# New step orders for all four stages of a state-space and gate kernel with its gradients

## The chip, the core and the metric

The kernel runs on one core of a Trainium2 chip. A core has five engines, each with its own queue of instructions that it works off in order: TensorE (PE in the profile; its weight loads are PEld), VectorE (DVE), ScalarE (ACT), GpSimd (POOL) and SyncE (SP, which here only issues transfers). They meet only at semaphores. TensorE writes its results to PSUM, and DVE or ACT must copy them out ("evict" them) before the bank can be used again. The metric is the device time of one execution in microseconds; the median of the runs counts.

## What is computed

The reference is a forward pass and its gradients. Cut to what matters:

```python
xn = layernorm(x)                              # x: [1, 2048, 512]
K[d, l] = Re sum_n C * exp(dt*A*l) * dt*B      # SSM kernel, 512 channels, 128 states, 2048 lags
s = causal_conv(xn, K) + xn * Dskip            # by FFT of length 4096
g = silu(silu(xn @ w1) @ w2)                   # w1: 512x1792, w2: 1792x512
out = x + s * g
# returned: out, and the gradients of sum(out * grad_out) with respect to
# x, A_re, A_im, B_re, B_im, C_re, C_im, log_dt, Dskip, w1, w2
```

## The kernel before

The program is unrolled and its schedule is manual: the order in which the Python code issues instructions is the order in which every engine's queue gets them. Four functions follow each other.

- **stage_1** (first step order): layer norm (`Setup.stats`, `.norm`, `.param`), the powers of exp(dt*A) (`power_phases`: X, XV, A, B, C, CC, S; B is three ACT passes, A and C are DVE work), and the two matrix products of the gate (`gen_ffn_fwd`). One step of the latter, an h step, makes 128x1024 of x@w1 in a PSUM tile ps_h, takes SiLU of it on ACT (aT) and copies it too (hs).
- **stage_2**: for four blocks b of channels, the tables of powers X and CY are loaded, copied on ACT (`copy_tables`, L869 and L870, step c) and multiplied out on DVE (`chunk_tables` and `quads`, L884 to L905, step g, five steps a block); TensorE makes K from them (`chunk_K`, step k, 4 a block), and transposes X (`gen_xt`, tile XT, step t, 11 a block). Beside that run the transform of xn (`spectrum`, step u: per half 8 steps of FA, a transpose on DVE (L162, 2 x 2.3 us), 8 steps of FX) and the transposes of w2 (step w, tile w2o). Step o opens the tables of a further block: transfers on the SP queue into the two table buffers, which have to be free. At its end K is stored (`store_K`), and stage_3 changes the PSUM banks and reads K again in another layout (`load_K`).
- **stage_3**: transforms of K and of the incoming gradient, their products, and the inverse transforms. DVE multiplies and transposes, ACT and DVE evict.
- **stage_5**: gradients of w2 (`Dw2`, step w, tile KXW), of h (`Bwd.dh`, step h, with the transposed result dhk), of x (`Bwd.dx`, step x), of the state tables (`Slabs`, step l: P2 twice, with the eviction Vb, then D3 on DVE, L1649 and L1652; the last step is P3, which needs the last D3), of w1 (`grads`, step m, tile o10b), the rest of the SSM gradients (`gen_ssm_final`, step f), and the output (`Out0`, step z). A z step issues on the SP queue the store of the tile before it, then three loads into the buffers of that pair (two of each), then computes on DVE (L1462, L1463).

The order inside a stage is written out by hand as strings, `SCORE_1`, `SCORE_2`, `SCORE_3` and `SCORE_5`. Each letter names a generator, and one letter runs it up to its next `yield`; a letter whose generator is used up does nothing. A capital letter runs the same step with `by_dve` set, and then the helper `ev` (L72 to L77) puts the eviction of that step, if it has one that goes through `ev`, on DVE and not on ACT:

```python
for ch in score:
    kk.by_dve = ch.isupper()
    next(parts[ch.lower()], None)
```

So a string fixes two things: the order in which the steps reach all the queues, and which engine evicts. Nothing else depends on it. Evictions by `ev` carry line 77 in the profile, whatever the tile. What is left of a generator at the end of a stage is run by `drain`.

Of the kernel before, what the change touches and what calls it, by code (L numbers as in the profile page):

```python
# [28 lines left out]
NU = 656  # L29


SCORE_1 = "pppppggppgppppppppgpggpppppppgppppgppgppgppppppppppgppppppppgppgpppgppppgpgpppppMgppppgppppppppgpppppgppmpgpmpppgpgppmpmpgpppgpgmppppgppmpMmgpgpmmpmggGmttgmtmGtgmtgggGgggGGg"
SCORE_2 = (
    "uuuuugutTTUKtTWuKuTtkTtgcTgtkgggttuuuoguttutcTkT",
    "Tgt",
    "TgktggkkotTguuuuuuuuwtuuuttUKkkWkttctwggugtuuutugtuWuTtTKkK",
    "kT",
)
SCORE_3 = (
    "TTu",  # L40
    "FkFFFFFfqfutqqqftfffqTFkfFnfDfkUfffffTDfffddFuddU",
    "aaafdkAffdddnaknDsdFadffafaFiDbbvBvvbvkddnsgksbadagasbgagFkdddGddaDqpijDbdpabaaadxxxiexvjepvtvvizzjgzBxjptgszxesgiggietxxzizizjzjbbbXfzyygbpsbbbeycbpxsyxzxxppsxsxxxelxcsjjzescszyselzsyzsyszlYzZZCCCCC",
)
SCORE_5 = (
    "uyuuwuuLlWWhywwWYuYYLwhllhwwllLlYHHWwlhLuyWll",
    "LyhwWYLYwlHYlylWLllwwywwllywylWHllywlwYllYWyLHwwwylylloYHoLoYlhoLHoolollhlYLxlhLxLLxxxllxxll",
    "zxHxzhzHxHxhxhfHxfxfxxxHhfxxHhttHftthxxxhfxzmxHxfxttxfxmxfttxftMzxtttxmttffffMtMmtzMffzzffmrtfmrzmrzmr",
)


# [43 lines left out]
def drain(k, parts, names):  # L94

    for n in names:
        for _ in parts[n]:
            pass
# [10 lines left out]
def play(kk, score, **parts):  # L109

    for ch in score:
        if ch == " ":
            continue
        kk.by_dve = ch.isupper()
        next(parts[ch.lower()], None)
    kk.by_dve = False
# [626 lines left out]
def stage_1(k):  # L743
# [58 lines left out]
    next(parts["g"])  # L802
    i = SCORE_1.index("t")
    play(k, SCORE_1[:i], **parts)
    drain(k, parts, "pm")
    play(k, SCORE_1[i:], **parts)
    drain(k, parts, "g")
# [1146 lines left out]
```

## Time and profile before

| | |
|---|---|
| median of 3 runs | 682.66 us (681.93 to 683.17) |
| profiled execution | 685.07 us, span of its instructions 683.0 us |
| mean granted TensorE clock | 0.957 |
| TensorE matmul, weight load | 83% and 49% of the span |
| DVE, ACT, POOL | 86%, 63%, 14% |
| transfers | 154.58 MB, 226 GB/s on average |

The span runs from the first to the last instruction. The busy share of an engine is an average over stages that have different limits, so the prediction reads the stages one by one: in the table by stretches, in the timeline of an engine (start and length of an instruction in us, and in brackets the idle time before it with what ended it), and in the groups of instructions (total us, mean ns of one, idle time before them).

### The profile page before, as it was taken

Reading aid. Unit: us, or ns where it says so; the run is one execution under the profiler, and the core shown is the slowest. Engines: PE = TensorE matmul, PEld = TensorE weight load, DVE = VectorE, ACT = ScalarE, POOL = GpSimd, SP = SyncE. Lnnn points to the kernel's source line nnn. Section 1 sums busy time; section 2 is a strip of 40 time slices with the busy share of each in tenths; the row PEclk is TensorE's granted clock in tenths of the full one; section 3 lists DMA queues with packets and bytes.
Section 4 is the critical chain, followed back from the end, with each engine's and each line's share of the span. In section 5 each row is a group of like instructions: output and inputs, shape, how many; then the busy total and the mean of one; then the engine's idle time right before and its main releaser. Section 6 shows DMA issues by size and latency. Waiting matters only on the chain. (4 is left out here: it accounts for less than half of the span.)

```text
span 683.0 us, 14339 instructions
## 1 busy us (share of the span) xinstructions
PE 565.2 (83%) x5668; PEld 336.6 (49%) x5668; DVE 586.6 (86%) x967; ACT 430.9 (63%) x524; POOL 95.4 (14%) x170
## 2 busy tenths in 40 slices
PE   2977978877577757789997858979998979999996
PEld 1433433346466546567775634445554434454553
DVE  5898999878999748998999988889998978989825
ACT  4899999965667826898989903373555244352321
POOL 1120000021001132112213051121211000000000
PEclk9999999999989899999999989999999999999998
DMA  8665757786878769956568689796969857976886
GB/s 255 215 214 202 262 216 262 247 287 203 257 232 269 236 181 243 294 206 194 177 214 211 173 254 225 215 271 153 263 181 224 183 188 209 265 231 197 250 291 203
DMA packets 173622, 154.58 MB, mean 226 GB/s; under 512 B 70574, under 2 KB 141750, under 8 KB 173556
## 3 DMA queue, kind: packets, MB, share of 16 engines
q1 hardware_dynamic: 157428, 112.70, 57.7%
q0 software_dynamic: 11920, 38.08, 18.1%
q10 hardware_dynamic: 4208, 2.89, 1.5%
q8 instruction: 44, 0.72, 0.4%
q14 instruction: 22, 0.18, 0.1%
HBM read 76.81 MB, written 67.65 MB: 212 GB/s over the span
## 5 line engine op out<-in xcount | busy, mean ns | idle before, releaser
L723 PE MATMUL ps_h<-XNT,W 128*128 128x512 bf16 x224 | 59.9, 419 | 21.7 <-ACT hs L77 14.9
L1739 PE MATMUL ps_da<-DOT,W2T 128*128 128x512 bf16 x224 | 54.6, 388 | 1.2 <-ACT Vb L77 1.2
L696 PE MATMUL ps_o<-W,aT 128*128 128x512 bf16 x224 | 52.4, 382 | 1.4 <-ACT aT L725 1.4
L1801 PE MATMUL ps_dx<-KXW,dhT 128*128 128x512 bf16 x224 | 52.6, 387 | 0.0
L1568 PE MATMUL ps_w<-DO_all,KXW 128*128 128x512 bf16 x224 | 51.0, 379 | 1.9 <-DMA XTl<-XTd 1.9
L723 PEld LDWEIGHTS <-W 128*128 128x128 bf16 x224 | 23.3, 105 | 53.3 <-issue 29.9
L1901 PE MATMUL ps_w<-dhc,xn 128*128 128x448 bf16 x256 | 49.1, 353 | 0.0
L77 ACT CAST Vb<-ps_V 128x1024 bf16<-128x1024 f32 x23 | 23.0, 1012 | 37.6 <-PE ps_V L1637 24.5
L77 ACT CAST FZ<-ps_i 128x1024 bf16<-128x1024 f32 x44 | 43.0, 1037 | 5.3 <-PE ps_i L187 5.0
L173 PE MATMUL ps_s<-FA,Wf 128*64 128x256 bf16 x384 | 36.1, 325 | 11.3 <-ACT FX L77 6.2
L1740 DVE TENSOR_TENSOR dhT<-ps_da,sd 128x1024 bf16<-128x1024 f32 x28 | 34.2, 1221 | 12.0 <-ACT sd L213 6.2
L77 ACT CAST FA<-ps_f 128x1024 bf16<-128x1024 f32 x39 | 37.9, 1054 | 9.2 <-PE ps_f L148 9.0
L1810 ACT ACTIVATE dxn<-dxn,c,rstd 128x512 f32<-128x512 f32 x16 | 13.0, 813 | 42.7 <-DVE c L1809 42.7
L1901 PEld LDWEIGHTS <-xn 128*128 128x128 bf16 x256 | 25.0, 98 | 23.7
L696 PEld LDWEIGHTS <-aT 128*128 128x128 bf16 x224 | 22.1, 99 | 29.4 <-issue 2.2
L1739 PEld LDWEIGHTS <-W2T 128*128 128x128 bf16 x224 | 21.5, 100 | 26.8 <-issue 5.1
L187 PEld LDWEIGHTS <-Vi 64*128 64x128 bf16 x576 | 27.7, 94 | 14.0 <-issue 4.2
L77 ACT CAST FX<-ps_s 128x1024 bf16<-128x1024 f32 x28 | 27.6, 1031 | 10.5 <-PE ps_s L173 5.1
L1360 PE MATMUL ps_v<-FZ,TI 128*128 128x256 bf16 x192 | 25.1, 281 | 10.8 <-DVE FZ L162 7.9
L1568 PEld LDWEIGHTS <-KXW 128*128 128x128 bf16 x224 | 21.2, 97 | 25.8 <-issue 2.8
L1801 PEld LDWEIGHTS <-dhT 128*128 128x128 bf16 x224 | 21.4, 99 | 25.0 <-issue 2.5
L173 PEld LDWEIGHTS <-Wf 128*64 128x64 bf16 x384 | 23.5, 118 | 19.9 <-issue 15.8
(313 smaller groups left out, 1452.8 us busy)
## 6 DMA issues: line engine op xcount, KB each, us to landing
XTd<-XT SPq DMA_DIRECT2D x20, 512.0 KB, 6.8
XP<-UXd POOLq DMA_DIRECT2D x16, 512.0 KB, 4.7
XTl<-XTd SPq DMA_DIRECT2D x31, 256.0 KB, 3.7
hTd<-hs SPq DMA_DIRECT2D x28, 256.0 KB, 3.5
aTd<-aT SPq DMA_DIRECT2D x28, 256.0 KB, 3.6
dhc<-dhd SPq DMA_DIRECT2D x16, 448.0 KB, 6.8
XYd<-XYg SPq DMA_DIRECT2D x25, 256.0 KB, 3.4
hsb<-hTd SPq DMA_DIRECT2D x18, 256.0 KB, 3.4
```

What stands on the lines that cost most here:

```text
L77: (k.nc.vector.tensor_copy if k.by_dve else k.nc.scalar.copy)(out=out, in_=in_)
L173: nc.tensor.matmul(out=ps[64 * h:64 * h + 64, c, j], lhsT=k.Wf[:, c, 0:64], rhs=A[:, 2 * (v + j) + h], start=True, stop=True)
L187: nc.tensor.matmul(out=ps[:, h, j], lhsT=Vc[z], rhs=y[z, c, v % 4 + j, :], start=(n == 0), stop=(n == len(Y) - 1))
L696: nc.tensor.matmul(out=pso[:], lhsT=aT[:, ft, tt * P:(tt + 1) * P], rhs=W2[:, ft, :], start=(ft == 0), stop=(ft == FT - 1))
L723: nc.tensor.matmul(out=ps[:, j], lhsT=W1[:, dk, ft * P:(ft + 1) * P], rhs=XNT[:, dk], start=(dk == 0), stop=(dk == DK - 1))
L1360: k.nc.tensor.matmul(out=ps[:, j], lhsT=k.TI[:, t0 + j, c, :], rhs=Z[:, 2 * (t0 + j) + c], start=(c == 0), stop=(c == 1))
L1568: nc.tensor.matmul(out=ps[:], lhsT=A[:, t, :], rhs=k.DO[:, t, :], start=(t == 0), stop=(t == T - 1))
L1739: nc.tensor.matmul(out=ps[:, j], lhsT=self.W2T[:, ft // 2, dk, j * P:(j + 1) * P], rhs=self.DOT[tc_][:, dk], start=(dk == 0), stop=(dk == ...
L1740: nc.vector.tensor_tensor(out=self.dhT[:, f0:f0 + 2, :], in0=ps[:], in1=sd[:], op=ALU.mult)
L1801: nc.tensor.matmul(out=psx[:], lhsT=dhT[:, ft, t % 4 * P:(t % 4 + 1) * P], rhs=self.W1T[:, ft, :], start=(ft == 0), stop=(ft == FT - 1))
L1810: nc.scalar.activation(out=dxn[:], in_=dxn[:], func=ACT.Identity, scale=k.rstd[:, t:t + 1], bias=c12[:, 0:1])
L1901: nc.tensor.matmul(out=ps[:], lhsT=k.xn[:, t, dk * P:(dk + 1) * P], rhs=ch[i][:, t, :], start=(t == 0), stop=(t == T - 1))
```

## The change

Only the strings are replaced. Every generator runs the same steps with the same tiles and the same transfers.

```diff
-SCORE_1 = "pppppggppgppppppppgpggpppppppgppppgppgppgppppppppppgppppppppgppgpppgppppgpgpppppMgppppgppppppppgpppppgppmpgpmpppgpgppmpmpgpppgpgmppppgppmpMmgpgpmmpmggGmttgmtmGtgmtgggGgggGGg"
+SCORE_1 = "pppppppppppppggpgpppGppgppppgppppgppppppgppppppgppgppgpppgppppggppppppppgppppgpMpgpppGpgpppppppgpgppppggpmpmmppppgppppgpppppgpppppppppgmgppmmpMgggGmmgttGmgmggmmmgGgggGmttGgt"
 SCORE_2 = (
-    "uuuuugutTTUKtTWuKuTtkTtgcTgtkgggttuuuoguttutcTkT",
-    "Tgt",
-    "TgktggkkotTguuuuuuuuwtuuuttUKkkWkttctwggugtuuutugtuWuTtTKkK",
-    "kT",
+    "guTuuuuuuuuwttTgtUKttkkgctgtttkggtotgtuuuttkTtgucttgktgtkgtkto",
+    "uT",
+    "uuuuutuKkuguuwukwtkctwgUugwuuggtutuutTuKtKTKk",
+    "ttT",
 )
 SCORE_3 = (
-    "TTu",
-    "FkFFFFFfqfutqqqftfffqTFkfFnfDfkUfffffTDfffddFuddU",
-    "aaafdkAffdddnaknDsdFadffafaFiDbbvBvvbvkddnsgksbadagasbgagFkdddGddaDqpijDbdpabaaadxxxiexvjepvtvvizzjgzBxjptgszxesgiggietxxzizizjzjbbbXfzyygbpsbbbeycbpxsyxzxxppsxsxxxelxcsjjzescszyselzsyzsyszlYzZZCCCCC",
+    "Tt",
+    "UFqFqFqkFFFffttqftfffqFnknuffDffffkfUfTuUDfffddFdn",
+    "kaaFadafdafdndkfdkDsdFdfaffafBvvDvAbbvidaddskbkgsabgagaFgdddGddDapijDpabdasadaixbxbvevjxtvvzjxtisgzpBjigpxgeggxtxzeizesxzzjbzzijiXfzbbyybbsepbpbsycsbxxcxpyxxpzxgsxxzejxezcljzqsylsesssyzyzzslYZZCsCCCC",
 )
 SCORE_5 = (
-    "uyuuwuuLlWWhywwWYuYYLwhllhwwllLlYHHWwlhLuyWll",
-    "LyhwWYLYwlHYlylWLllwwywwllywylWHllywlwYllYWyLHwwwylylloYHoLoYlhoLHoolollhlYLxlhLxLLxxxllxxll",
-    "zxHxzhzHxHxhxhfHxfxfxxxHhfxxHhttHftthxxxhfxzmxHxfxttxfxmxfttxftMzxtttxmttffffMtMmtzMffzzffmrtfmrzmrzmr",
+    "wuuuyuuwlWWywwhYlwLYllYylywylyllwwullwlhhwlhlwL",
+    "YLlHlWwYulyLhylwhyllwlwwYhwLyYYLwwlhylwlwyWLHwwlWloYlhHlolLhyloLoooloyhllYxlllLhxLlxlxxlx",
+    "xzxxHzhhzxxhhxHfHxfxxxhxHxhxthftHtthxxxhzxxxfhxtmtttzfftfxxftmtmtMxftmmfffxMxxttfftfzmMfzzfmffmrtrrmrzz",
 )
```

Many capitals stand on steps without an eviction of that kind (a transpose, a product, a used-up generator). Counted step by step, these evictions are on DVE:

| evictions on DVE | before | after |
|---|---|---|
| stage_1: hs | 0 | 2 |
| stage_2 and the first string of stage_3: XT | 16 | 8 |
| stage_2: w2o | 3 | 0 |
| stage_2: Kout | 1 | 1 |
| stage_2: FA and FX of xn | 1 | 1, and one FX at the head of stage_3 |
| rest of stage_3: XT; FA, FX and FZ of the other transforms | 2; 16 | 1; 15 |
| stage_5: dhk, Vb, KXW, YTl, o10b | 15, 9, 7, 12, 4 | 8, 6, 3, 10, 3 |

In stage_2 the five products of a block keep their order. In the new string the second transpose of xn stands ahead of the long product of the last block (`quads`) and behind the short one; before it stood ahead of both, with the ACT copies of that block between. Of the capitals that act ahead of the last product of the last block, the old string has 11 XT, 2 w2o, 1 FA and 1 Kout, the new one 4 XT and 1 FX. In stage_1 the new string runs 13 power and norm steps before the first h step, the old one 5. At the end of the first part of stage_5 the new string puts two x steps between the last D3 and P3. In the last string, the z step of tile 8 has nine m steps behind it in both orders. The last two x steps, with the result of x that they make DVE and SP store, stood four m steps ahead of it and now stand right ahead of it; three of the four loads of the last chunk of dh and two stores of the SSM gradients (step f) stand between them and it.

## The prediction, on record before the result

> **What bounds the kernel now.** I read the page's head first, then the table by stretches, then the timelines of the engines where a stretch has idle time. The page says that two engines are near the top, and which work each evicts. Its columns after the span are busy us, share and count.
>
> ```profile
> span 683.0 us, 14339 instructions
> PE 565.2 (83%) x5668; PEld 336.6 (49%) x5668; DVE 586.6 (86%) x967; ACT 430.9 (63%) x524; POOL 95.4 (14%) x170
> ```
>
> Shares over the whole span do not say which engine sets the end of a stage. The table by stretches does (length, then busy us of PE, PEld, DVE, ACT, POOL, granted clock, DMA share, GB/s):
>
> ```profile
> 34.00:51.00 17.00, 12.63 (x52) 5.21 (x51) 16.51 (x34) 17.00 (x23) 3.73 (x3) 0.90 0.61 212
> 165.00:218.00 53.00, 36.73 (x932) 30.55 (x934) 51.59 (x82) 35.29 (x40) 4.73 (x8) 0.90 0.90 268
> 218.00:250.00 32.00, 22.20 (x509) 17.95 (x502) 18.00 (x33) 20.21 (x23) 6.60 (x12) 0.84 0.65 189
> 290.00:391.00 101.00, 90.14 (x1137) 68.40 (x1136) 97.64 (x87) 91.59 (x99) 21.41 (x35) 1.00 0.67 196
> 408.00:553.00 145.00, 129.70 (x1290) 68.15 (x1283) 131.41 (x197) 66.74 (x75) 22.66 (x41) 0.99 0.89 211
> 553.00:676.00 123.00, 120.52 (x679) 60.35 (x677) 91.13 (x167) 44.63 (x70) 0.55 (x1) 0.99 0.78 238
> ```
>
> Four regimes. Stage_1 runs on ACT, with no idle time in 34 to 51. Stage_2 runs on DVE: 51.6 of 53 us, while ACT has 17.7 us free. Stage_3 has DVE, ACT and PE all near the top. In stage_5 PE and DVE are coupled until 553 (15.3 us of PE idle), and from there PE is full (2.5 us idle). So work taken off DVE should pay in stage_2 and somewhat in stage_5 before 553, and not at all after it.
>
> **Stage_2, the largest term.** What an eviction costs on either engine (count, total us, mean ns, idle before):
>
> ```profile
> L77 ACT COPY XT<-pt_xt 128x1024 bf16<-128x1024 bf16 x22 | 22.3, 1040 | 10.8 <-PE pt_xt L1012 5.8 <-DMA XTd<-XT 3.8 <-DMA XYc<-XYd 1.3
> L77 DVE COPY XT<-pt_xt 128x1024 bf16<-128x1024 bf16 x18 | 11.8, 683 | 10.3 <-PE pt_xt L1012 10.2
> L77 DVE CAST FA<-ps_f 128x1024 bf16<-128x1024 f32 x9 | 10.5, 1215 | 3.4 <-PE ps_f L148 3.4
> 166.70 0.84 DVE L77 CAST Kout<-ps_k 128x656 bf16<-128x656 f32 x1 [1.02 <-PE ps_k L938]
> ```
>
> Stage_2 ends with K, and the last K steps wait for the last product of the last table. Ahead of that product the old order has 11 XT, 2 w2o (same shape, so the same 683 ns), one FA and one Kout on DVE: 13 x 0.683 + 1.215 + 0.84 = 10.9 us. The new one has 4 XT and an FX of the FA's shape: 4 x 0.683 + 1.22 = 3.95 us. That is 7.0 us less. The DVE timeline adds a wait, and the PE timeline shows what hangs on the product (start, us, and the idle time in brackets; one row of the groups between):
>
> ```profile
> 223.60 3.57 DVE L884 TENSOR_TENSOR m<-CY 128x1536 bf16<-128x1536 bf16 x4 [2.22 <-ACT CY L870]
> L162 DVE STREAM_TRANSPOSE FA<-FA 128x2048 f32<-128x2048 f32 x12 | 27.0, 2293 | 0.8 <-ACT FA L77 0.8
> 234.19 0.28 DVE L905 TENSOR_TENSOR X<-m 128x256 bf16<-128x256 bf16 x1
> 235.02 3.43 PE L938 MATMUL ps_k<-X,CY 128*32 128x41 bf16 x179
> 249.76 1.47 PE L148 MATMUL ps_f<-DS,TF 128*128 128x256 bf16 x12 [1.94 <-ACT w2o L77]
> ```
>
> DVE waited 2.2 us for the ACT copy of the last block's CY; in the new order the transpose of xn (twice the 2293 ns below) stands behind the short product, just ahead of the one that needs the copy, so this wait should go. Together 9.2 us at most. Against it: the seven copies now queue on ACT at 1.04 us, in one queue with CY copies that wait for transfers; and the table buffers still come free by K and the transposes, so DVE may reach a block before its tables have landed (no row shows a landing time that was not waited for). The other end is therefore nothing. Nearest is the row of the stretch: ACT busy 35.3 of 53, so about 10 us more fit, but the last transpose now waits for a run of ACT evictions. I take half, **-4.6 us**. At the bank change PE starts again only when the last ACT eviction is done (249.76, 1.94 us of wait). The new order puts one FX behind it and takes three transposes from ahead of K to behind it; I cost this at nothing, hidden by the K reload that runs then.
>
> The Trainium skill speaks against this: TensorEngine Tiling (Array Packing), section PSUM Bottleneck, advises both ScalarE and VectorE for evacuation. By it the shift buys little, as each bf16 copy is 0.36 us longer on ACT in the rows above; the rows agree on that price, and only the 17.7 us that ACT has free speak for the shift here.
>
> **Stage_1.** The queue of ACT is the bound from here on:
>
> ```profile
> 20.69 1.02 ACT L725 ACTIVATE aT<-ps_h 128x1024 bf16<-128x1024 f32 x1 [2.68 <-PE ps_h L723]
> 26.41 0.63 ACT L607 COPY ex<-lam 128x512 f32<-128x512 f32 x1
> 28.30 0.69 DVE L362 SCALAR_TENSOR_TENSOR b_f<-tau,b_r 128x512 f32<-128x512 f32 x1
> L77 ACT CAST hs<-ps_h 128x1024 bf16<-128x1024 f32 x28 | 30.7, 1096 | 0.0
> ```
>
> Two hs go to DVE: -2 x 1.10 us. The first power pass on ACT (0.63 and another 0.63 behind it, 1.2 us of queue) moves ahead of the first h step, into the idle time before 20.69: -1.2. But the first B pass now stands behind the third h step and needs b_f, ready at 28.99, while ACT is done with three h steps at 26.4: +2.6. Sum **-0.8 us**. Bounds: -3.4 without that gap; above, one pair of A and C on DVE (2 x 0.42 + 2 x 0.69 + 2 x 1.24 = 4.7 us, the rows next):
>
> ```profile
> L361 DVE TENSOR_SCALAR b_r<-tau 128x512 int32<-128x512 f32 x22 | 9.3, 424 | 0.4
> L643 DVE TENSOR_TENSOR XYg<-ex,b_w 128x1024 bf16<-128x1024 f32 x8 | 9.9, 1238 | 1.9 <-ACT b_w L629 1.9
> ```
>
> if ACT has to wait for it where the new order strings power steps together without an h step between.
>
> **Stage_3.** On DVE one FA and two XT fewer and one FX more: -1.4 us of 97.6. The rest is a new sequence of the same work, all three engines over 89% busy. I take 0, with -1.4 and +2.5 (a wait like the 1.94 above at a second place) as ends.
>
> **Stage_5 before 553.** The last D3 holds PE through P3:
>
> ```profile
> 551.25 0.39 PE L1667 MATMUL ps_S<-T,Sel 128*32 128x512 bf16 x2 [3.34 <-DVE T L1649]
> 551.85 0.39 PE L1667 MATMUL ps_S<-T,Sel 128*32 128x512 bf16 x2 [0.21 <-DVE T L1652]
> 552.45 0.39 PE L1667 MATMUL ps_S<-T,Sel 128*32 128x512 bf16 x2 [0.20 <-DVE T L1652]
> 544.71 3.19 PE L1801 MATMUL ps_dx<-KXW,dhT 128*128 128x512 bf16 x14
> L77 ACT COPY dhk<-pt_dh 128x1024 bf16<-128x1024 bf16 x13 | 13.1, 1009 | 25.6 <-DMA dhd<-dhk 10.8 <-DVE Gbd L1624 7.1 <-PE pt_dh L1755 4.9
> L77 DVE COPY dhk<-pt_dh 128x1024 bf16<-128x1024 bf16 x15 | 10.2, 682 | 2.8 <-DMA dhd<-dhk 2.8
> ```
>
> The new order has two x steps (14 matmuls, 3.2 us) between that D3 and P3, so these 3.75 us are covered. Ahead of this point 13 evictions leave DVE; six are bf16 copies (4 dhk, 2 YTl) that hold PSUM 0.33 us longer on ACT, and I let all of these 2.0 us show. **-1.75 us**, ends -3.75 and 0. After 553 PE is full, so nothing more comes.
>
> **The tail.** PE ends at 675.8, the span 7.2 us later; between lies the chain of z steps on SP:
>
> ```profile
> 636.61 39.51 PE L1901 MATMUL ps_w<-dhc,xn 128*128 128x448 bf16 x208
> 636.38 0.46 SPq L91 DMA_DIRECT2D out_dram<-zS  x1
> 642.02 0.32 SPq L1450 DMA_DIRECT2D zS<-Sd  x1
> 653.98 0.34 SPq L91 DMA_DIRECT2D out_dram<-zS  x1
> 664.55 0.69 DVE L1462 TENSOR_TENSOR zS<-zS,zg 128x1024 bf16<-128x1024 bf16 x1 [8.91 <-DMA zg<-gd]
> 680.21 0.27 PE L1082 MATMUL pt_row<-ident_bfloat,ob 128*4 128x128 bf16 x1 [4.09 <-DVE ob L1545]
> ```
>
> The z step of tile 8 reaches SP at 653.98, and 26.2 us later DVE is done. An m step is 39.2/13 = 3.0 us of PE, so nine of them put x's old distance in figures: x ended at 636.6, z's slot came 17.4 us later. In the new order x ends only nine m steps, 27.2 us, before PE's end, and the slot must come behind it. With 6.5 us (x's layer norm on DVE, two stores of step f, three loads) the end is -27.2 + 6.5 + 26.2 + 2.8 = 8.3 us behind PE, **+1 us** against 7.2; with the old lag of 17.4 us it is +12. Ends 0 and +12; I take +1, because the old lag held a whole z step (5.6 us from store to next load) and three chunk loads that now lie ahead of x.
>
> **Sum.** -4.6 - 0.8 + 0 - 1.75 + 1 = -6.15 us: the profiled execution of 685.07 us (span 683.0) would become 678.9, and the median of 682.66 becomes **676.5 us**.
>
> One more rule: in TensorE: Matmul & The Clock Gate, Part 1, the skill says that the array falls to half rate after some 3.4 us of idle time until activity returns. The row of 218 to 250, clock 0.84 with a PE that waits, agrees; by it the sum gains at most 0.16 x 22.2 = 3.6 us more if those waits go, an estimate that I leave out.
>
> **The rivals.** *SP's tail decides (slower).* If z's slot keeps 17.4 us behind x, the tail costs +12 in place of +1: 687.5. It ends slower than before once the lag is over 12.7 us. For it: SP's queue is in order and each z holds it; against: fewer entries lie between. *ACT gates stage_2 (slower).* The CY copy of each of three blocks waits on ACT for its transfer, with K and the XT copies that free the next table buffer behind it. At the head of stage_5 and of stage_2 ACT shows such waits:
>
> ```profile
> ACT Y L1035 <- DMA XYy<-XYd: 19.1, 1, 19.1
> ACT CY L869 <- DMA XYc<-XYd: 7.0, 2, 5.6
> ```
>
> Three of 5.6 us are +16.8, less the 9.2: +7.6 in place of -4.6, so 688.7; it turns slower when these waits pass some 11 us together. Against it: 7.0 us in all before. *The bank change eats it.* DVE ends stage_2 early, but the reload of K and stage_3 start as before: -0.8 - 1.75 + 1, 681.1.
>
> **How the numbers follow.** Forecast 0.52; SP's tail 0.18; ACT 0.14; bank change 0.16, which lies at the edge of what can be told from no change (about 0.2%, 1.4 us), so half of it counts as the same. Faster 0.60, same 0.08, slower 0.32. The range goes from 667 (-9.2 - 3.4 - 1.4 - 3.75 is 664.9, not all at once) to 689 (both slower rivals).
>
> **What would show it.** Right: the last product of stage_2 (L905) ends 3 to 7 us before 234.5; DVE copies of XT are 9 and not 18; no wait of 3 us before the last P3; PE over 97% busy in its last 120 us; the end 7 to 10 us behind PE's last m step. Wrong: ACT waits over 10 us for XYc in stage_2; DVE idle before the first product of a block (L901, for X); z's slot on SP over 13 us behind the last x; the first TensorE work of stage_3 no earlier than 249.8.

## The result, and the profile after

The changed kernel takes 681.04 us (median of 20 runs) and the kernel before 683.57 (20 runs beside them): a ratio of 0.9967, with a 95% interval of 0.9954 to 0.9981. That is 2.3 us faster, where 6.15 us were forecast. All ratios below are to runs of the kernel before on the same chip; in us they are taken on 683.6.

The profiled execution of after took 682.6 us (span 680.8). Its page has less work on DVE (586.6 before) and more on ACT (430.9 before):

```profile
span 680.8 us, 14322 instructions
PE 571.8 (84%) x5668; PEld 339.3 (50%) x5668; DVE 570.1 (84%) x940; ACT 453.6 (67%) x551; POOL 96.0 (14%) x170
```

The evictions moved as the strings say: in the groups of instructions by shape, DVE copies 9 XT in place of 18, and two hs are there (total us, mean ns, idle time before them).

```profile
L77 ACT COPY XT<-pt_xt 128x1024 bf16<-128x1024 bf16 x31 | 31.1, 1040 | 8.1 <-PE pt_xt L1012 3.1 <-issue 2.3 <-DMA K_b<-Kud 1.6
L77 ACT CAST hs<-ps_h 128x1024 bf16<-128x1024 f32 x26 | 27.6, 1061 | 0.0
L77 DVE COPY XT<-pt_xt 128x1024 bf16<-128x1024 bf16 x9 | 6.1, 682 | 6.0 <-ACT Kout L77 4.2 <-PE pt_xt L1012 1.8
L77 DVE CAST hs<-ps_h 128x1024 bf16<-128x1024 f32 x2 | 2.4, 1224 | 7.4 <-DMA aTd<-aT 5.5 <-ACT aT L725 1.9
```

Where the time went shows when fixed points of the program are set side by side (start in us from the head of the span, read off the timelines of their lines). The last four columns are runs of the next section.

| | before | after | new stage_1 only | new stage_2 only | new stage_5 only | new 2 and 5 |
|---|---|---|---|---|---|---|
| last product of the gate (L696) | 146.7 | 155.0 | 152.4 | 145.8 | 146.8 | 146.5 |
| first transform of xn (L148) | 151.5 | 161.3 | 162.0 | 150.3 | 152.1 | 151.3 |
| last table product (L905) | 234.2 | 239.3 | 244.0 | 227.1 | 234.2 | 228.7 |
| reload of K (L977) | 251.8 | 257.1 | 260.7 | 244.5 | 250.9 | 245.7 |
| first KXW product (L1568) | 404.7 | 410.0 | 412.9 | 396.9 | 405.3 | 398.0 |
| last P3 (L1667) | 552.5 | 548.5 | 560.2 | 544.8 | 541.7 | 535.2 |
| last m step (L1901) | 675.8 | 675.3 | 684.3 | 667.7 | 668.5 | 661.2 |
| span | 683.0 | 680.8 | 692.9 | 674.7 | 675.2 | 668.4 |

After is 9.8 us late when the transform of xn begins. From there stage_2 takes 78.0 us to its last product in place of 82.7; from the first KXW product stage_5 takes 265.3 us to the last m step in place of 271.1. So the terms that were forecast as gains are there, and stage_1, forecast at -0.8 us, takes most of them back.

Three places stand out in stage_1 of after; in before, from 20 us on, DVE has no wait over 1.8 us there. The DVE timeline, then PE's, then DVE's again at the end of the stage (start, us, idle time before it and what ended it):

```profile
32.73 1.22 DVE L77 CAST hs<-ps_h 128x1024 bf16<-128x1024 f32 x1 [1.87 <-ACT aT L725]
...
89.70 1.23 DVE L77 CAST hs<-ps_h 128x1024 bf16<-128x1024 f32 x1 [5.52 <-DMA aTd<-aT]
...
137.32 0.69 DVE L72 TENSOR_TENSOR DS<-G,g 128x1024 bf16<-128x1024 bf16 x1
...
146.73 1.23 DVE L643 TENSOR_TENSOR XYg<-ex,b_w 128x1024 bf16<-128x1024 f32 x1 [7.58 <-DMA XYd<-XYg]
```

```profile
34.01 2.29 PE L723 MATMUL ps_h<-XNT,W 128*128 128x512 bf16 x5 [4.62 <-DVE hs L77]
...
86.63 1.89 PE L723 MATMUL ps_h<-XNT,W 128*128 128x512 bf16 x8 [0.65 <-ACT hs L77]
```

The first hs on DVE holds a bank for which TensorE waits 4.62 us. At the second, DVE stands 5.52 us; the trace names a store, but the tile that it evicts is only made by the product at 86.63 (done at about 88.5) and read by ACT's aT up to 89.7, when the eviction begins; so DVE was simply there too early. At the end, C10, the last power product (L643), waits 7.58 us for a table buffer. The SP timeline shows why:

```profile
132.10 0.32 SPq L727 DMA_DIRECT2D hTd<-hs  x1
138.04 0.33 SPq L691 DMA_DIRECT2D G<-in_grad_out_dram  x1
138.42 0.43 SPq L731 DMA_DIRECT2D aTd<-aT  x1
138.90 1.00 SPq L634 DMA_DIRECT2D XYd<-XYg  x2
140.96 0.32 SPq L727 DMA_DIRECT2D hTd<-hs  x1
...
144.72 5.19 SPq L634 DMA_DIRECT2D XYd<-XYg  x4
```

SP issues nothing from 132.4 to 138.0. It stands at a load of G, whose buffer is read by the DS product at 137.32, and on DVE that product is behind the product of C9. So the store of C8's table, which was complete at 131.2, is issued at 138.9, and C10 needs that buffer.

### The profile page after: what moved, and what is told of

Its sections match the earlier page's. It is cut to its first block, busy times and chain, and to the rows that moved or that the text cites. A ratio compares the mean times of both kernels' runs of the same rounds, so it can differ in the third digit from the quotient of the medians.

```text
span 680.8 us, 14322 instructions
## 1 busy us (share of the span) xinstructions
PE 571.8 (84%) x5668; PEld 339.3 (50%) x5668; DVE 570.1 (84%) x940; ACT 453.6 (67%) x551; POOL 96.0 (14%) x170
## 5 line engine op out<-in xcount | busy, mean ns | idle before, releaser
L696 PE MATMUL ps_o<-W,aT 128*128 128x512 bf16 x224 | 55.3, 397 | 3.1 <-ACT aT L725 3.1
L1739 PE MATMUL ps_da<-DOT,W2T 128*128 128x512 bf16 x224 | 52.8, 379 | 1.1 <-DMA dhd<-dhk 0.9
L1568 PE MATMUL ps_w<-DO_all,KXW 128*128 128x512 bf16 x224 | 53.2, 391 | 0.0
L1901 PE MATMUL ps_w<-dhc,xn 128*128 128x448 bf16 x256 | 49.2, 353 | 0.0
L696 PEld LDWEIGHTS <-aT 128*128 128x128 bf16 x224 | 22.7, 102 | 33.0 <-issue 5.3
L77 ACT CAST Vb<-ps_V 128x1024 bf16<-128x1024 f32 x26 | 26.0, 1016 | 19.1 <-PE ps_V L1637 14.7
L77 ACT COPY dhk<-pt_dh 128x1024 bf16<-128x1024 bf16 x20 | 20.1, 1007 | 27.0 <-DMA dhd<-dhk 17.8
L77 ACT COPY XT<-pt_xt 128x1024 bf16<-128x1024 bf16 (+1 forms) x35 | 32.5, 967 | 8.1 <-PE pt_xt L1012 3.1
L1901 PEld LDWEIGHTS <-xn 128*128 128x128 bf16 x256 | 25.0, 98 | 23.7
L1568 PEld LDWEIGHTS <-KXW 128*128 128x128 bf16 x224 | 21.4, 100 | 26.7 <-issue 5.4
```

What stands on the lines that cost most here:

```text
L77: (k.nc.vector.tensor_copy if k.by_dve else k.nc.scalar.copy)(out=out, in_=in_)
L696: nc.tensor.matmul(out=pso[:], lhsT=aT[:, ft, tt * P:(tt + 1) * P], rhs=W2[:, ft, :], start=(ft == 0), stop=(ft == FT - 1))
L1568: nc.tensor.matmul(out=ps[:], lhsT=A[:, t, :], rhs=k.DO[:, t, :], start=(t == 0), stop=(t == T - 1))
L1739: nc.tensor.matmul(out=ps[:, j], lhsT=self.W2T[:, ft // 2, dk, j * P:(j + 1) * P], rhs=self.DOT[tc_][:, dk], start=(dk == 0), stop=(dk == ...
L1901: nc.tensor.matmul(out=ps[:], lhsT=k.xn[:, t, dk * P:(dk + 1) * P], rhs=ch[i][:, t, :], start=(t == 0), stop=(t == T - 1))
```

## The experiments

"Old" and "new" strings are those of the change's diff; in the short diffs OLD_1 and NEW_1 stand for the two strings of SCORE_1, and so on.

**One stage back.** From the kernel after, one stage at a time gets its old string.

```diff
-SCORE_1 = NEW_1
+SCORE_1 = OLD_1
```

> The kernel after, with the old step order in stage_1 alone. Theory A (stage_1 pays by itself): in the trace of after stage_1 reaches the first product of stage_2 some 13 us later, and from the first transform of xn on it is 8.4 to 9.8 us behind before; the rest of the kernel gains about 11 us on its own. Then this run takes 681.0 - 8 to 10 = 671 to 673 us, some 1.6% under the kernel before, and the last L905 ends at 230 to 231. Theory B (the gain of stage_2 is only the late start): the last product of stage_2 is set by transfers and by TensorE whatever the start, so a faster stage_1 is waited away; then the last L905 stays at 237 to 239 and the run takes 679 to 681 us.

Measured: 0.9806 (0.9774 to 0.9837), 672.4 us, the last L905 at 227.1. Theory A holds, B falls: with the old first string the rest of the change takes 13.3 us off, and that version is well ahead of both kernels.

```diff
-SCORE_2 = NEW_2
+SCORE_2 = OLD_2
```

> The kernel after, with the old step order in stage_2 alone. Theory A: stage_2 loses the 8 us that it gained (from the first xn transform on 4.7 us), so 686 to 689 us, slower than before. Theory B: the stretch shrank because it began later, so the old order with the late start takes about as long as the new one: 681 to 683 us.

Measured: 1.0037 (1.0015 to 1.0059), 687.4 us, the last L905 at 244.0 in place of 239.3. Theory A, though by the ratios the order is worth 4.8 us here and not 8. That is less than the 7.1 us that it is worth alone (below); the traces have 4.7 and 7.1 at the last L905, but the intervals of the ratios alone would not part the two.

```diff
-SCORE_3 = NEW_3
+SCORE_3 = OLD_3
```

> The kernel after, with the old step order in stage_3 alone. If the new order of stage_3 costs the 3.5 us by which its stretch grew between the two traces, this run takes 677.5 us. If the stretch grew only because stage_2 now leaves one transform and three transposes more to it, or because its transfers fall otherwise, the old order doesn't help: 680 to 682 us.

Measured: 0.9964 (0.9945 to 0.9984), 682.4 us beside 684.1 of before; after has 0.9967. The order of stage_3 is worth nothing that can be told. The 3.5 us by which its stretch grew (from its first transform, at 249.8 and 251.6, to the first KXW product) are not its own: from the reload of K on, the stretch is 152.9 us in before and in after.

```diff
-SCORE_5 = NEW_5
+SCORE_5 = OLD_5
```

> The kernel after, with the old step order in stage_5 alone. If stage_5 gained the 5.8 us of TensorE time and the 1.7 us of tail by its own order, this run takes 688 to 689 us. If most of the 9.3 us gained ahead of the last P3 is given back later whatever the order (TensorE is full in the last 120 us and only the sum of work counts), then 683 to 685 us.

Measured: 1.0064 (1.0041 to 1.0087), 689.3 us. Stage_5's order is worth 6.6 us by the ratios; the second reading falls.

**One stage alone.** The same question from the other side, on the kernel before.

```diff
-SCORE_1 = OLD_1
+SCORE_1 = NEW_1
```

> The kernel before with the new step order in stage_1 alone. If the price of the new stage_1 is its own, as 0.9967 against 0.9806 with all else new says, this run is at 1.013 to 1.019 of before (+9 to +13 us). If the old stage_2 takes a part of it up, because it waits for other things at its start, it is at 1.004 to 1.010.

Measured: 1.0136 (1.0107 to 1.0164), +9.3 us. The price is stage_1's own.

```diff
-SCORE_2 = OLD_2
+SCORE_2 = NEW_2
```

> The kernel before with the new step order in stage_2 alone (all else old). The trace with the old first string has the last L905 7.1 us earlier than before. If that is stage_2's own gain and stage_3 passes it on, 0.988 to 0.992 of before. If only the new stage_3 can use it, 0.995 to 1.0. The prediction had -4.6 us, 0.993.

Measured: 0.9896 (0.987 to 0.9921), -7.1 us. The table above shows the 7.1 us at the last L905 and 7.3 at the reload of K: the bank change and stage_3 pass them on.

```diff
-SCORE_5 = OLD_5
+SCORE_5 = NEW_5
```

> The kernel before with the new step order in stage_5 alone. By the stretches of the traces (first L1568 to TensorE's last m step: 271.1 us before, 264.9 with the old first string) 0.988 to 0.993 of before. The prediction had -1.75 + 1 us, 0.999; if the gain hangs on the stages ahead, it is there, 0.997 to 1.0.

Measured: 0.9892 (0.9865 to 0.9919), -7.4 us, the tail included.

```diff
-SCORE_2 = OLD_2
-SCORE_5 = OLD_5
+SCORE_2 = NEW_2
+SCORE_5 = NEW_5
```

> The new step order in stage_2 and stage_5 alone, stage_1 and stage_3 as before. If the new order of stage_3 is worth nothing, as the run with the old one beside a new stage_1 says, this is 0.978 to 0.983 of before, as with the new stage_3. If it costs some 3.5 us, as the stretch in the trace of after suggests, 0.974 to 0.977; if it gains, 0.984 to 0.990.

Measured: 0.9804 (0.9778 to 0.9829), 670.3 us: the fastest version here, the same as with the new stage_3. Alone, the three orders give +9.3, -7.1 and -7.4 us, -5.2 together; after has -2.3. The 2.9 us between are about what the intervals of three ratios leave open (each some 2 us).

**What in stage_1 costs.** From the kernel after, first the two effective G as g (fragments of SCORE_1):

```diff
-pppppppppppppggpgpppGppgppppg
+pppppppppppppggpgpppgppgppppg
...
-gpMpgpppGpgppppppp
+gpMpgpppgpgppppppp
```

> The kernel after, with the two hs evictions of stage_1 back on ScalarE and every step where it is. With the old first string the kernel took 8.7 us less than after, so that is what the whole new string of stage_1 costs; this run asks for the share of the two evictions. Theory A1 (a held PSUM bank and a held DVE): in after TensorE waited 5.6 us for them and DVE stood 5.5 us on the second one's buffer: this run takes 4 to 6 us less than after, 675 to 677 us. Theory A2 (the order of the steps is what costs): the two evictions only move 2.2 us to ScalarE, which had no idle time then, and the run is within 1.5 us of after, 680 to 682.5 us.

Measured: 0.9903 (0.9874 to 0.9932), 4.4 us better than after. The size is A1's, but half of A1's reason falls, as PE's timeline of this run shows:

```profile
33.00 3.49 PE L723 MATMUL ps_h<-XNT,W 128*128 128x512 bf16 x8 [5.06 <-ACT hs L77]
```

With the first hs on ACT, TensorE waits as long at the same place, for ACT; and the kernel before has a wait of nearly that length a little later:

```profile
41.29 3.33 PE L723 MATMUL ps_h<-XNT,W 128*128 128x512 bf16 x8 [3.94 <-ACT hs L77]
```

Most of the gain comes at the second hs. Ahead of it ACT is 0.8 us earlier in this run than in after (the aT at 87.80 and at 88.58), behind it 2.5 us (the next aT, at 92.94 and 95.44), and 5.4 us at the next power copy (103.67 and 109.11), before which ACT in after waits 2.75 us for the store of a table. ACT's timeline in after, and in this run:

```profile
88.58 1.09 ACT L725 ACTIVATE aT<-ps_h 128x1024 bf16<-128x1024 f32 x1
92.09 1.34 ACT L648 CAST XYg<-b_w 128x1024 bf16<-128x1024 f32 x1 [2.42 <-DVE b_w L646]
```

```profile
87.80 1.09 ACT L725 ACTIVATE aT<-ps_h 128x1024 bf16<-128x1024 f32 x1
88.71 1.09 ACT L77 CAST hs<-ps_h 128x1024 bf16<-128x1024 f32 x1
89.60 1.44 ACT L648 CAST XYg<-b_w 128x1024 bf16<-128x1024 f32 x1
```

In after the power product of C5 (L646, b_w) stands on DVE behind the eviction, which waits for its tile, and ACT waits for C5. With the eviction on ACT, DVE does C5 in that time, and ACT goes on without a gap although it does one eviction more.

Then the last two h steps earlier:

```diff
-gpppppppppgmgppmmp
+gppppppgpppgmppmmp
```

> The kernel after, with the last two h steps of stage_1 earlier: one ahead of the power steps A10, C9, B10 and one right behind these, ahead of the mask step, as they stand in before; all else is as in after. In after the nine power steps stand in a string ahead of these two h steps, and the last power product waited 7.6 us on DVE for the store of a table buffer, which was behind their stores on SP. Theory A3 (that chain costs): the last product comes some 5 us earlier, the tables of block 0 land earlier, and the run takes 676 to 678 us. Rival: the end of stage_1 hangs on TensorE and ScalarE, the wait on DVE is covered, and the run takes 680 to 682 us.

Measured: 0.9908 (0.9875 to 0.994), 4.0 us better than after: A3. SP issues the load of G without a wait and the store of C8's table 6.3 us earlier than in after, and the first table product of stage_2 (L901) begins at 147.1 in place of 153.9. The SP and DVE timelines of this run:

```profile
131.68 0.38 SPq L691 DMA_DIRECT2D G<-in_grad_out_dram  x1
132.12 0.44 SPq L731 DMA_DIRECT2D aTd<-aT  x1
132.61 1.97 SPq L634 DMA_DIRECT2D XYd<-XYg  x2
```

```profile
140.15 1.23 DVE L643 TENSOR_TENSOR XYg<-ex,b_w 128x1024 bf16<-128x1024 f32 x1 [2.42 <-ACT b_w L629]
```

Both edits together:

> The kernel after, with both edits of the two runs before: hs on ScalarE and the last two h steps earlier. If these two are the cost of the new stage_1, the run comes to 672 to 674 us, as with the old first string. If the rest of the new order (13 power and norm steps ahead of the first h step, strings of power steps between the h steps) costs as well, it stays 3 us or more above, 676 to 679 us.

Measured: 0.9838 (0.9813 to 0.9863), 8.8 us better than after (674.6 us, beside 685.1 of before), and 2.2 us above the run with the old first string, which lies within the intervals. The two are nearly all that stage_1 costs. The 13 power steps ahead of the first h step cost at most the rest.

**Is it the relief of DVE?** Four runs part the two things that a string does, the order and the engine of each eviction. The first two have the new order of a stage (old first string) with the evictions that DVE had before: the n-th step of a kind is capital where the n-th was in the old string. Of stage_2, its first and third string and the first of stage_3:

```diff
-    "guTuuuuuuuuwttTgtUKttkkgctgtttkggtotgtuuuttkTtgucttgktgtkgtkto",
+    "gutuuuuuUuuWTTtgTuKTtKkgcTgtTtkggtotgtuuuttkTTgucTtgkTgtkgtkTo",
...
-    "uuuuutuKkuguuwukwtkctwgUugwuuggtutuutTuKtKTKk",
+    "uuuuutuKkuguuwukWtkctwgUugWuuggtutuuttuKtkTKk",
...
-    "Tt",
+    "TT",
```

> The kernel after with the old first string (672.4 us), in which stage_2 keeps its new order but evicts the same tiles on DVE as before: 11 XT, 2 w2o, 1 FA and 1 Kout ahead of the last product in place of 4 XT and 1 FX. Theory R (the relief of DVE is the gain): these 7.0 us come back in full or nearly so, 677.5 to 679.5 us. Theory O (the place of the transpose of xn and the other moves are the gain, and ScalarE would have been as late): within 2 us of that kernel, 671 to 674.5 us.

Measured: 1.0003 (0.9978 to 1.0028), 13.5 us more than 0.9806. Theory O falls, but R's price is only half of it. The waits of DVE in stage_2 (us in total, times, longest) show where the rest can come from: it now waits for the X tables of two blocks (0.6 us in the run with the old first string) and for a tile of FA that TensorE had not made (no such wait there).

```profile
DVE m L901 <- DMA X<-XYd: 8.1, 2, 4.5
DVE FA L77 <- PE ps_f L148: 4.2, 1, 4.2
```

The reverse, old order with the new string's evictions on DVE, in the kernel before (first string of stage_2):

```diff
-    "uuuuugutTTUKtTWuKuTtkTtgcTgtkgggttuuuoguttutcTkT",
+    "uuuuuguTttuKTtwukuttkttgctgtkgggttUuuoguttutcTkt",
```

> The kernel before, in which stage_2 keeps its old order but evicts on DVE what the new string evicts there (4 XT and 1 FX ahead of the last product). Theory R (relief of DVE pays by itself, 7.0 us fewer in DVE's queue): 0.989 to 0.993 of before, and the last L905 ends 5 to 7 us ahead of 234.5. Theory C (which tile goes to which engine pays only together with its place in the order, as the old tiles in the new order cost 13 us and not 7): no gain, 0.998 to 1.01.

Measured: 1.0026 (0.9999 to 1.0053), the last L905 at 234.2 as before: theory C. The busy us of the engines in 151 to 227 (columns as before: length, PE, PEld, DVE, ACT, POOL, clock, DMA share, GB/s), first in this run, then with the new order alone, then in the kernel before:

```profile
151.00:227.00 76.00, 51.91 (x1184) 42.73 (x1182) 63.86 (x105) 61.73 (x71) 8.31 (x14) 0.91 0.80 238
```

```profile
151.00:227.00 76.00, 55.70 (x1228) 44.36 (x1227) 70.38 (x120) 65.14 (x75) 10.68 (x18) 0.93 0.84 254
```

```profile
151.00:227.00 76.00, 52.13 (x1190) 43.01 (x1189) 70.72 (x115) 53.76 (x61) 8.31 (x14) 0.90 0.81 242
```

In the old order DVE is relieved by 6.9 us and turns them into waits: it waits 6.2 us for FA evictions that are now late on ACT. In the new order it stays as busy as before (70.4 us) and gets 120 instructions done in place of 115. The waits of DVE in stage_2 of the run with the old order:

```profile
DVE FA L162 <- ACT FA L77: 6.2, 2, 3.2
DVE m L884 <- ACT CY L870: 3.5, 2, 2.4
DVE XT L77 <- PE pt_xt L1012: 2.1, 1, 2.1
```

The same pair for stage_5 (the edit shown by the start of the second string), first the new order with the old evictions on DVE:

```diff
-    "YLlHlWwYulyLhylwhyllwlwwYhwLyYYLww
+    "YllHlWwYuLylhylWhyllwlwwyHwlyYYlwW
```

> The kernel after with the old first string (0.9806 of the kernel before), in which stage_5 keeps its new order but evicts the same tiles on DVE as before (15 dhk, 9 Vb, 7 KXW, 12 YTl, 4 o10b in place of 8, 6, 3, 10, 3). With the old strings of stage_5 the kernel after took 6.6 to 8.2 us more. Theory R (DVE's relief is that gain): 0.988 to 0.992 of before, 5 to 8 us more than with the new capitals. Theory O (the order is the gain): within 2 us of it, 0.979 to 0.984.

Measured: 0.999 (0.9966 to 1.0014), 12.6 us more than 0.9806, more than either theory had. Up to the last P3 TensorE waits 4.3 us for D3 (L1649), in place of 1.3 us in the run with the old first string; the rest was not taken apart. Then the old order with the new evictions:

```diff
-    "LyhwWYLYwlHYlylWLllwwywwllywylWHll
+    "lyhwWyLYwLhYlylwlLlwwywwllywYlwhLL
```

> The kernel before, in which stage_5 keeps its old order but evicts on DVE what the new strings evict there (17 evictions fewer). Theory R: the gain of stage_5 comes by itself, 0.990 to 0.994 of before. Theory C (only together with the order): no gain, 0.998 to 1.005.

Measured: 1.0334 (1.0298 to 1.037), 22.8 us slower with 17 evictions fewer on DVE. Neither theory had that. About half of it is one capital, in PE's timeline and DVE's:

```profile
682.61 1.65 PE L1901 MATMUL ps_w<-dhc,xn 128*128 128x448 bf16 x4 [11.73 <-DVE o10b L77]
```

```profile
673.54 0.69 DVE L1462 TENSOR_TENSOR zS<-zS,zg 128x1024 bf16<-128x1024 bf16 x1 [10.06 <-DMA zg<-gd]
...
678.68 0.69 DVE L1462 TENSOR_TENSOR zS<-zS,zg 128x1024 bf16<-128x1024 bf16 x1 [3.72 <-DMA zg<-gd]
...
681.95 0.61 DVE L77 CAST o10b<-ps_w 128x448 bf16<-128x448 f32 x1
```

An o10b of 0.6 us stands on DVE behind two z steps, which wait for the loads of SP's tail, and TensorE waits for its bank 11.7 us. Most of the rest stands ahead of the last P3, which starts at 561.0 and not 552.5. There TensorE waits 4.3 us for a KXW and 2.9 us for a dhk on ACT, two waits that before doesn't have; what they cost was not tried.

**The cover of P3.** In the run with the old first string, the two x steps go behind P3 (end of the second string of stage_5):

```diff
-YxlllLhxLlxlxxlx
+YxlllLhxLlxllxxx
```

> The kernel after with the old first string, in which P3 stands right behind the last D3 and the two x steps that stood between come behind it. The prediction gave these two steps 3.75 us, TensorE's wait for the last D3. If that is so, 0.985 to 0.987 of before (3 to 4 us more than 0.9806). Rival: in the new order DVE is no longer late there, and TensorE, full afterwards, has the same sum of work: within 1 us, 0.979 to 0.982.

Measured: 0.9869 (0.9836 to 0.9902), 0.63% or 4.3 us more than with the cover, where the two intervals leave open some 1 to 7 us; by the traces, from the first L1568 to the last m step, 1.9 us. So the cover pays about what it was priced at, or somewhat less. PE's timeline has the wait back, and the table by stretches of 2 us shows what follows it (PE busy is the second number, the clock the one after POOL):

```profile
536.35 1.22 PE L1667 MATMUL ps_S<-T,Sel 128*32 128x512 bf16 x4 [2.37 <-DVE T L1649]
```

```profile
534.00:536.00 2.00, 0.00 (x0) 0.00 (x1) 1.35 (x2) 1.04 (x2) 0.00 (x0) 1.00 0.07 15
536.00:538.00 2.00, 1.65 (x8) 0.32 (x7) 1.50 (x3) 0.00 (x0) 0.00 (x0) 0.53 0.00 0
538.00:540.00 2.00, 2.00 (x8) 0.78 (x7) 0.00 (x0) 0.58 (x1) 0.55 (x1) 0.62 0.00 0
```

## Why the prediction was right in sign and wrong in size

- **Stage_1, "Sum -0.8 us", is the step that failed: +9.3 us**, outside its bound of +4.7. It counted what each queue does more or less (two hs, one power pass, one wait for b_f) and bounded the rest by one pair of A and C. It asked what ACT saves by an hs that leaves it, not how long that hs stands on DVE and what stands behind it there: the two cost 4.4 us, most of it at the second. And it named nothing that stands behind the new string of nine power steps at the end of the stage, on DVE and then on SP: 4.0 us. The power steps ahead of the first h step, from which its -1.2 and +2.6 came (ACT's wait for b_f is 1.3 us in after), cost at most the rest.
- **Stage_2, -4.6 us: it measured -7.1**, inside its range and in the place foretold, the end of the last product; the wait for CY, 2.2 us before, is 0.2 in after and 1.5 with only stage_2 new. The mechanism was half right. The evictions that leave DVE are needed (13.5 us are lost when they come back), but 7.0 us less in DVE's queue is not a price: in the old order the same relief gave nothing.
- **ACT as the bound of stage_2** did not come about: in after it waits 0.3 us for XYc at the three later blocks, where over 10 would have shown that rival.
- **Bank change and stage_3, 0: right.** 7.1 us at the last product are 7.3 at the reload and 7.8 at the first KXW product. The sign set for a failure (stage_3 starts no earlier than 249.8; after has 251.6) came up, but because of stage_1 ahead of it.
- **Stage_5, -1.75 + 1: it measured -7.4.** The cover of P3 is there and pays: after has no wait of a microsecond before the last P3. Its price of 3.75 us lies between the 1.9 us of the traces and the 4.3 us of the ratios, though it left out the clock behind the wait: in before that is 0.71, 0.50 and 0.94 in the three stretches of 2 us from 552 on, about 1.7 us of TensorE time (an estimate from these rows).

```profile
552.00:554.00 2.00, 1.80 (x9) 0.51 (x5) 0.40 (x1) 0.58 (x1) 0.24 (x1) 0.71 0.95 316
554.00:556.00 2.00, 2.00 (x6) 0.76 (x5) 0.03 (x1) 0.00 (x0) 0.31 (x1) 0.50 0.99 305
556.00:558.00 2.00, 2.00 (x14) 1.02 (x13) 1.93 (x6) 0.30 (x1) 0.00 (x0) 0.94 0.90 333
```

The rest of the term was too small, because the +2.0 us for copies that hold PSUM longer did not show, and because waits ahead of P3 went that no term named (in before 1.9 us for a load of XTl and 1.3 us for a KXW on DVE, among others). For the balance, take the two rows of before and the two of the run with only stage_5 new, cut at the last P3: ahead of it TensorE's idle time falls from 16.2 to 8.4 us, where the wait priced at 3.75 us is less than half of the fall, and its busy time by 3.7; behind it both rise, by 2.0 and 1.5. From the first KXW product to the last m step that is -7.9.

```profile
404.70:552.50 147.80, 131.61 (x1307) 68.90 (x1304) 134.50 (x201) 66.62 (x74) 22.66 (x41) 0.99 0.89 215
552.50:675.80 123.30, 120.82 (x681) 60.51 (x680) 90.93 (x166) 44.75 (x70) 0.55 (x1) 0.99 0.78 238
```

```profile
405.30:541.70 136.40, 127.95 (x1293) 67.39 (x1290) 119.08 (x175) 75.55 (x85) 22.65 (x41) 0.99 0.87 227
541.70:668.50 126.80, 122.28 (x695) 61.84 (x694) 95.46 (x177) 49.73 (x77) 0.55 (x1) 1.00 0.78 239
```

- **The tail, +1: it measured -0.5** (6.7 us behind the last m step in the run with only stage_5 new, 5.5 in after, 7.2 before). The lag of z's slot behind x was foretold at 6.5 us and is 6.1 in after (x's last products end at about 648.3): the rival of SP's tail, at over 12.7 us, is out. The sign of the end, 7 to 10 us behind the last m step, did not come either: after ends 5.5 us behind it.

```profile
654.38 1.19 SPq L91 DMA_DIRECT2D out_dram<-zS  x1
```

- **PE over 97% busy in its last 120 us**: 96.2% (115.4 us). Nearly, and with no effect on the sum.

So three of four stages went the way that was foretold or better, and the sum came out at a little over a third of the forecast because two errors partly cancel: -13.4 us from stages 2 and 5 where -5.35 were expected, and +9.3 from stage_1 where -0.8 was. With stage_1 as measured and the other terms as forecast the kernel would have become about 4 us slower, so the right sign is luck.

## What to carry to other kernels

An eviction that is moved to another engine takes a place in that engine's queue, and its price is not its duration: ask how long it stands there for its tile, what stands behind it, and what it stands behind (5.5 us for 1.2 here, 11.7 us for 0.6 there). So the engine of an eviction and its place in the order are one choice: in both stages either half of the new string without the other gave nothing or cost up to 23 us (other choices of the same number of evictions were not tried). And where a trace names a wait, ask what would be waited for next: TensorE's 4.62 us for a DVE eviction became 5.06 us for ACT.

## What the runs showed of the hardware

A short wait of TensorE can cost more than its length. After 2.37 us without a matmul (the rows of the last experiment) the granted clock was 0.53 and 0.62 in the next 4 us, and a pair of P3 matmuls took 0.61 us; with the cover it takes 0.38. In after, the product of the gate waits 2.19 us at the end of stage_1, where TensorE had 0.6 us of work in the last 3.7 us; then it runs at half the clock until past 148. Timeline and stretches:

```profile
142.88 12.32 PE L696 MATMUL ps_o<-W,aT 128*128 128x512 bf16 x43 [2.19 <-ACT aT L725]
```

```profile
140.00:144.00 4.00, 1.72 (x5) 0.55 (x6) 0.00 (x0) 4.00 (x7) 1.11 (x2) 0.74 0.99 278
144.00:148.00 4.00, 4.00 (x11) 1.38 (x10) 1.27 (x2) 1.68 (x4) 0.00 (x0) 0.50 1.04 389
148.00:150.00 2.00, 2.00 (x9) 0.87 (x8) 1.91 (x9) 0.59 (x2) 1.11 (x1) 0.82 0.65 245
```

Not every such wait does it. At one place of stage_5, ahead of the transposes of L1047, TensorE waits 2.38 us in the run with only stage_5 new and 2.37 us in the run with the old first string. Behind it the first has half the clock and the second the full one; the stretch that begins about a microsecond behind the wait, in the first and in the second:

```profile
432.00:434.00 2.00, 2.00 (x19) 0.75 (x12) 1.97 (x5) 1.97 (x2) 0.50 (x1) 0.50 0.91 309
```

```profile
426.00:428.00 2.00, 2.00 (x26) 1.03 (x24) 1.97 (x5) 1.85 (x2) 0.50 (x1) 1.00 0.97 323
```

The Trainium skill (TensorE: Matmul & The Clock Gate, Part 1) has the half rate after about 3.4 us of idle time. These waits were shorter, and the half rate came behind some of them all the same, for some 3 to 6 us. What decides whether it comes, no run here shows.
